# Two of the first weight loads issued from ScalarE's queue, behind a small copy that calls for its table

## The chip, the cores and the metric

The kernel runs on one core of a Trainium2 chip. The metric is the device time of one execution in microseconds, lower is better; three runs of the kernel before are shown, and one more execution with the hardware profiler on. In the profile the engines are called PE (TensorE, matmuls), PEld (TensorE's weight loads), DVE (VectorE), ACT (ScalarE), POOL (GpSimd) and SP (SyncE, which here only issues transfers); SPq is SyncE's instruction queue.

## The reference

Two branches over the same x (2048 x 512, fp32) are mixed row by row with a sigmoid gate. Branch A is a two-dimensional Fourier transform written as matmuls, of which the real part is kept. Branch B is a gated unit with a ReLU gate.

```python
def reference(A_x, A_dft_seq_re, A_dft_seq_im, A_dft_hid_re, A_dft_hid_im, B_x, B_W_gate, B_W_up, B_W_down, gate_w):
    ...
        a = jnp.einsum("bsd,ed->bse", x, dft_hid_re)
        b = jnp.einsum("bsd,ed->bse", x, dft_hid_im)
        y = jnp.einsum("ts,bse->bte", dft_seq_re, a) - jnp.einsum("ts,bse->bte", dft_seq_im, b)
    ...
        gate = jnp.einsum("bsd,df->bsf", x, W_gate)
        up = jnp.einsum("bsd,df->bsf", x, W_up)
        gate = gate * (lambda x, dt: x.astype(dt))(gate > 0, gate.dtype)
        h = gate * up
        return jnp.einsum("bsf,fd->bsd", h, W_down)
    ...
    g = _sigmoid((x * gate_w).sum(-1, keepdims=True))
    ...
    return g * a + (1 - g) * b
```

Here W_gate and W_up are 512 x 1792, W_down is 1792 x 512, and the sequence matrices are 2048 x 2048.

## The kernel before

**Arithmetic.** Each fp32 operand is split into a high part (a cast to the fp32r type) and a low part (the difference), and a product is three matmuls: high by low, low by high, high by high (`PARTS`). Most products of 2 x 2 blocks are formed with seven block products in place of eight (the tables `LEFT`, `RIGHT` and `ORDER`); the tile names carry the number of the product or of the block. In the head, product 1 needs the block "11" of x and the first column half of a weight set, product 2 the block "21" and the second column half; the products 5, 6, 3, 7, 4 need sums of blocks.

**Stages.** The matmuls that form the hidden layer come first (weight sets c = 0 to 6, each for 128 columns in both halves of gate and up, and two halves q of the rows), then the transform along the hidden dimension, then the transform along the sequence together with the down projection. The change lies in the first few microseconds.

**The planner.** Engines run their instructions in program order, and the kernel's own planner (`Plan`) writes that order. Each operation is recorded as a `Step` with a key, the number of the matmul it belongs to. `due` works back from the matmuls to a latest time of each step; `order` (line 191) then plays the steps through in its own figures: 0.5 us for an issue on SyncE or ScalarE (`ISSUE`), one line on which transfers move one behind another at 0.175/16 us for each 4 KB (1.4 us for 512 KB), landing 2.5 us behind that (`LANDING`), a cast on ScalarE 0.19 us and 0.845 ns an element, 0.035 us for a wait (`WAIT`). A transfer issued between 2.3 and 2.9 us is counted 2.3 times (`COLD`). SyncE's and ScalarE's steps are looked through some 48 deep, VectorE's and ScalarE's sorted by due time: the first that can start is taken, unless a later one can start more than 0.12 us earlier (line 224). Line 255 sorts everything by the planned start, and that is the program. Whatever the chip does, an engine then waits for its steps in this order.

**Who issues what.** `load` (line 356) issues from SyncE, `store` and `accumulate` from GpSimd. ScalarE issues no transfer. `Weights.load` (line 413) loads raw weights, half `h`, column half `n`, depth half `k`; `a_hi` (416) casts them on ScalarE into `wah`, `a_lo` (419) forms `wal` on VectorE.

**The head** (from line 1230). `warm_up` clears `gs` on VectorE (128 x 64) and runs 18 matmuls on constants. The loads are recorded, and issued by SyncE, in this order: x "11" first depth half, weight set 0 first column half and first depth half, x "11" second depth half, set 0 first column half and second depth half, set 1 first column half (both depth halves in one), x "21" whole, set 0 second column half, set 1 second column half, x "12", the other halves of the weights, x "22" and the gate's weights. On the chip a cast of a weight piece waits for its load. TensorE's order is fixed: 12 matmuls of product 1 on set 0 (six on the first depth half, six on the second), 12 of product 1 on set 1, then product 2 on set 0 and on set 1, then the others. Product 2 on a set adds into the bank of product 1, so it also waits until ScalarE has copied that bank (`evac`, the ACT COPY of 128 x 1024).

Of the kernel before, what the change touches and what calls it, by code (L numbers as in the profile page):

```python
# [8 lines left out]
F32 = mybir.dt.float32  # L9
# [5 lines left out]
P = 128  # L15
# [113 lines left out]
class Plan:  # L129
# [3 lines left out]

    MATMUL, WAIT, LANDING, COLD = 0.22667, 0.035, 2.5, 2.3

    ISSUE = {"sync": 0.5, "scalar": 0.5, "gpsimd": 0.9}

    REST = 60
# [5 lines left out]
    def op(self, key, f, *a):  # L144
        self.ops.append((key, len(self.ops), f, a))
# [45 lines left out]
    def order(self):  # L191
        todo = {}
        for s in self.steps:
            todo.setdefault(s.engine, []).append(s)
        for e in ("vector", "scalar"):
            todo[e].sort(key=lambda s: s.due)
        free = dict.fromkeys(todo, 0.0)
        late, line, live, ends = 0.0, 0.0, 0, []
        left = {b: len({id(x) for x in b.uses}) for b in self.bufs if b.kind == "unit"}
        done, begun, now = [], set(), 0.0  # L200

        turn = {s: n for n, s in enumerate(self.steps)}
        ahead = sorted(min(turn[s] for s in b.uses) for b in left if b.uses)
        while any(todo.values()):
            best = None
            for e, queue in todo.items():
                found = None
                near = queue[:1] if e == "tensor" or not queue else [*queue[:48], min(queue, key=turn.get)]
                for s in near:
                    if any(x.start is None for x in s.after):  # L210
                        continue
                    t = max(free[e], now)
                    for x in s.after:
                        t = max(t, x.end + (0 if x.engine == e else self.WAIT + 0.16 * (x.engine == "tensor")))
                    if e != "tensor":
                        t = max(t, (s.key - self.AHEAD[e]) * self.MATMUL + late)
                    new = {r.base for r in (*s.writes, *s.reads) if r.base.kind == "unit" and r.base not in begun}
                    if new:
                        short = live + bisect_left(ahead, turn[s]) + len(new) - UNITS
                        if short > 0:  # L220
                            if len(ends) < short:
                                continue
                            t = max(t, ends[short - 1])
                    if found is None or t < found[0] - 0.12:
                        found = t, s, new
                if found and (best is None or found[0] < best[0]):
                    best = found
            if best is None:
                raise ValueError(f"no way on at {len(done)}: {[(e, q[0].key, q[0].name) for e, q in todo.items() if q]}")
            t, s, new = best  # L230
            now = t
            while ends and ends[0] <= t:
                ends.pop(0)
                live -= 1
            live += len(new)
            for b in new:
                ahead.remove(min(turn[x] for x in b.uses))
            begun |= new
            todo[s.engine].remove(s)
            s.start = t  # L240
            if s.name == "dma_start":
                free[s.engine] = t + self.ISSUE[s.engine]
                line = max(line, free[s.engine]) + s.work * (self.COLD if 2.3 < t < 2.9 else 1)
                s.end = line + self.LANDING + (2.0 if "accum_op" in s.k else 0)
            else:
                s.end, free[s.engine] = t + s.work, t + s.hold
            if s.engine == "tensor" and s.key >= 0:
                late = max(late, t - s.key * self.MATMUL - 6 * self.MATMUL)
            for b in {r.base for r in (*s.writes, *s.reads) if r.base.kind == "unit"}:
                left[b] -= 1  # L250
                if not left[b]:
                    ends.append(max(x.end for x in b.uses))
                    ends.sort()
            done.append(s)
        self.steps = sorted(done, key=lambda s: s.start - 0.2 * (s.engine == "scalar"))
# [23 lines left out]
def kernel(ctx: ExitStack, tc, xP, xG, wgu, wd, cr, ci, wri, gw, out):  # L279
# [22 lines left out]
    small = ctx.enter_context(tc.tile_pool(name="small", bufs=1))  # L302

    plan = Plan()
    op, pe = plan.op, plan.pe
# [10 lines left out]

    gs = Buf(plan, "gs", [2, 32], kind="fixed", tile=small.tile([P, 2, 32], F32, name="gs"))

    gx = Buf(plan, "gx", [2, 32], kind="fixed", tile=small.tile([P, 2, 32], F32, name="gx"))

    def buf(name, shape=(2, N), dtype=F32):
# [22 lines left out]
    def E():  # L344
        return plan

    def mm(ps, w, x, start=False, stop=False):
        plan.tensor.matmul(ps, w, x, start=start, stop=stop, skip_group_check=True)
# [7 lines left out]
    def load(o, i):  # L356
        plan.sync.dma_start(o, i)
# [15 lines left out]
    def x_load(q, b, ks=slice(0, 2)):  # L373
        k, j, o = int(b[0]) - 1, int(b[1]) - 1, piece[q, b]
        return lambda: load(o[:, ks], xP[2 * q + j, k, :, ks])
# [26 lines left out]
    class Weights:  # L402
# [7 lines left out]
            self.d = buf("wd", [2, 2, 2, P], F32R)  # L410
            self.b = [[buf(f"wb{h}{x}", [2, 2, 2, P], F32R) for x in "hl"] for h in range(2)]

        def load(self, h, n=slice(0, 2), k=slice(0, 2)):
            load(self.raw[h][:, n, k], wgu[self.c, h, :, n, k])

        def a_hi(self, n=slice(0, 2), k=slice(0, 2)):
            E().scalar.copy(self.a[0][:, n, k], self.raw[0][:, n, k])
# [268 lines left out]
    def gate_store():  # L686
        for n in range(2):
            E().vector.transpose(gx[:, n], gs[:, n])
            for i in range(0, P, 32):
                load(gd[n, :, i:i + 32], gx[i:i + NT * KD, n])  # L690
# [376 lines left out]
    class Joint:  # L1067
# [5 lines left out]
        def __init__(self, ms, banks, x=2, raw=None, last=False, lead=(0, 0), own=()):  # L1073
            self.ms, self.banks, self.x, self.lead, base, wide = ms, banks, x, lead, plan.now, 12 * len(ms)
            self.w, self.c, self.s = {}, {}, buf("js")
            self.o = [buf(f"jo{p}") for p in range(2)]
            self.g = gate_row(0, (x - 2, x), base + 10)
            for n, m in enumerate(ms):
                self.lefts(m, base + 12 * n - lead[1], raw, wide)
            self.v = [buf("jv0"), buf("jv1", (N,))] if last else None  # L1080
            made = {(m, hh): self.sums(m, hh, base + 6 * hh - lead[1]) for m in own for hh in range(2)}
            if last:
                op(base - 40, lambda: load(self.v[0].all, od[x - 2, :, 0:2]))
                op(base + 20, lambda: load(self.v[1].all, od[x, :, 1]))
            order = [(y, m) for y in ORDER_Z for m in ms]
            if last:
                order[-4:] = [(y, m) for m in ms for y in ORDER_Z[-2:]]
            for n, (y, m) in enumerate(order):
                for hh in range(2):
                    self.right(m, y, hh, base + 12 * n + 6 * hh, made.get((m, hh)))  # L1090
            for y, m in order:
                for hh in range(2):
                    pe(6, self.product, m, y, hh)
                if m == ms[-1]:
                    self.evac(y, plan.now)
                elif last and y == 4:
                    op(plan.now, lambda: E().scalar.copy(self.half(1), self.bank(4, HALVES[1])))
# [131 lines left out]

    def warm_up():  # L1230
        E().vector.memset(gs.all, 0.0)
        for n in range(WARM):
            half = slice(n % 2 * (N // 2), (n % 2 + 1) * (N // 2))
            mm(ps8[:, (2, 3, 6, 7)[n // 2 % 4], half], ones[:, :P], ones, start=n in (0, 2, 4, 6), stop=True)

    NP = KF // 2
    ws = [Weights(c) for c in range(2)]
# [4 lines left out]
    halves, whole = [slice(0, 1), slice(1, 2)], slice(0, 2)  # L1242
# [6 lines left out]
    def w_half(w, n, k=whole):  # L1249
        w.a_hi(n, k)  # L1250
        w.a_lo(n, k)

    op(-100, warm_up)
    for k in halves:
        op(-99, x_load(0, "11", k))
        op(-99, ws[0].load, 0, halves[0], k)
    op(-99, ws[1].load, 0, halves[0])
    op(-99, x_load(0, "21"))
    for w in ws:
        op(-99, w.load, 0, halves[1])  # L1260
    op(-98, x_load(0, "12"))
    for w in ws:
        op(-98, w.load, 1)
# [11 lines left out]
    for n, m in enumerate((5, 6, 3, 7, 4)):  # L1275
# [3 lines left out]
        for w in ws:  # L1279
# [3 lines left out]
            else:  # L1283
                h, i = divmod(SLOT[m], 2)
# [28 lines left out]
    def prepared(c, ahead=66):  # L1313
        w = Weights(c)
        w_prep(w, plan.now, ahead)
        return w

    for c in range(2, NP):
        w = prepared(c)
# [123 lines left out]
```

## Time and profile before

| | |
|---|---|
| median of three runs | 779.66 us (779.49, 779.66, 781.6) |
| the profiled execution | 779.72 us |
| its span in the profile | 777.9 us |
| granted TensorE clock, mean | 0.999 |
| PE busy | 772.3 us, 99% of the span, 3414 matmuls |
| DVE busy | 665.5 us, 86%, 736 instructions |
| ACT busy | 425.9 us, 55%, 499 instructions |
| POOL busy | 121.5 us, 16%, 178 instructions |
| moved by the DMA engines | 205.65 MB, mean 264 GB/s |

The span runs from the first to the last instruction; the time of the execution has about 1.8 us around it. The profile's rows give a start and a duration in microseconds, the engine, the line of the kernel, the operation, and the tiles written and read (buffer numbers left out); what stands in brackets is how long the engine had been idle before, and what released it. Since the planner issues every instruction, all have line 126, and the tile names tell them apart. Matmuls are pipelined and overlap in the rows, so their pace is read from start to start. A view of the transfers gives for each load its size and the time from issue to landing.

### The profile page before, as it was taken

What the parts mean: (1) busy time and instruction counts of PE and PEld (TensorE: products, weight loads), DVE (VectorE), ACT (ScalarE), POOL (GpSimd) and SP (SyncE); (2) the same over time, 40 slices, a digit from 0 to 9 for tenths busy, and PEclk for the clock granted to TensorE, in tenths of its full rate; (3) what the DMA queues carried; (4) which work ended last, traced back from release to release, by engine and by line L of the source; (5) the groups of instructions that cost most, each with busy time, mean ns of one, the idle gap of its engine ahead of it and who ended that gap; (6) DMA issues with size and microseconds to landing.
All of it is one profiled execution on the core that took longest, in us unless ns stands there. A gap on an engine that the chain in (4) does not pass through costs nothing.

```text
span 777.9 us, 9558 instructions
## 1 busy us (share of the span) xinstructions
PE 772.3 (99%) x3414; PEld 638.3 (82%) x3414; DVE 665.5 (86%) x736; ACT 425.9 (55%) x499; POOL 121.5 (16%) x178
## 2 busy tenths in 40 slices
PE   9999999999999999999999999999999999999997
PEld 7888888888888888888888888888888888888886
DVE  6999766766778685999996999998699899699898
ACT  6666444434455443566653667547644755345791
POOL 0021333332222332211000000030002011001000
PEclk9999999999999999999999999999999999999999
DMA  9246497999897999775369789989989997999982
GB/s 324 82 150 163 162 267 227 314 300 251 229 322 281 337 408 405 276 279 187 94 208 380 267 262 389 373 172 266 310 294 206 356 306 167 284 250 305 388 278 55
DMA packets 60255, 205.65 MB, mean 264 GB/s; under 512 B 7152, under 2 KB 7664, under 8 KB 60208
## 3 DMA queue, kind: packets, MB, share of 16 engines
q1 hardware_dynamic: 37264, 122.72, 43.5%
q0 software_dynamic: 22944, 82.32, 39.2%
q8 instruction: 27, 0.44, 0.2%
q14 instruction: 20, 0.16, 0.1%
HBM read 155.45 MB, written 74.73 MB: 296 GB/s over the span
## 4 chain that ended last, share of the span: by engine, by line
PE 98%; DMA 1%; SPq 0%; ACT 0%; DVE 0%; issue 0%; DVEq 0%
PE ps L126 98%; DMA x<-xP 1%; SPq L126 0%; DVE jo L126 0%; ACT xh L126 0%; ACT wah L126 0%; DVEq L126 0%
## 5 line engine op out<-in xcount | busy, mean ns | idle before, releaser
L126 PE MATMUL ps<-ch,ll 128*128 128x512 f32 x516 | 200.7, 389 | 0.0
L126 PE MATMUL ps<-cl,lh 128*128 128x512 f32 x516 | 200.7, 389 | 0.0
L126 PE MATMUL ps<-ch,lh 128*128 128x512 f32 x516 | 200.7, 389 | 0.0
L126 ACT CAST ch<-r 128x1024 fp32r<-128x1024 f32 x80 | 82.1, 1054 | 74.1 <-DVE r L126 64.6
L126 PEld LDWEIGHTS ps<-ch,ll 128*128 128x128 f32 x516 | 96.9, 188 | 20.1
L126 PEld LDWEIGHTS ps<-cl,lh 128*128 128x128 f32 x516 | 96.9, 188 | 20.1
L126 PEld LDWEIGHTS ps<-ch,lh 128*128 128x128 f32 x516 | 96.9, 188 | 20.0
L126 DVE TENSOR_TENSOR cl<-r,ch 128x1024 fp32r<-128x1024 f32 x80 | 95.6, 1221 | 7.7 <-ACT ch L126 6.1
L126 ACT CAST ch<-hr 128x1024 fp32r<-128x1024 f32 (+1 forms) x56 | 51.8, 945 | 43.5 <-DVE hr L126 21.2
L126 DVE TENSOR_TENSOR jcl<-jc,jch 128x1024 fp32r<-128x1024 f32 x56 | 65.6, 1222 | 7.8 <-issue 3.9
L126 ACT COPY s<-ps 128x1024 f32<-128x1024 f32 (+1 forms) x52 | 46.0, 884 | 47.6 <-PE ps L126 46.3
L126 ACT CAST jch<-jc 128x1024 fp32r<-128x1024 f32 x56 | 56.2, 1052 | 16.1 <-PE ps L126 14.0
L126 DVE TENSOR_TENSOR cl<-hr,ch 128x1024 fp32r<-128x1024 f32 (+1 forms) x56 | 60.1, 1087 | 5.1 <-ACT lh L126 2.7
L126 ACT ACTIVATE ps<-ps 128x512 f32<-128x512 f32 (+1 forms) x42 | 33.0, 785 | 55.0 <-PE ps L126 52.6
L126 POOL DMA_DIRECT2D out<-z x20 | 14.6, 729 | 297.3 <-DVE z L126 290.0
L126 DVE TENSOR_TENSOR r<-r,r 128x1024 f32<-128x1024 f32 x48 | 57.6, 1220 | 0.2
L126 DVE TENSOR_TENSOR u<-ps,s 128x1024 f32<-128x1024 f32 x28 | 34.1, 1221 | 13.4 <-PE ps L126 8.8
L126 POOL DMA_DIRECT2D hd<-h x35 | 23.0, 662 | 136.9 <-DVE h L126 125.6
L126 PE MATMUL ps<-xh,wb0l 128*128 128x512 f32 x112 | 43.8, 391 | 0.0
L126 PE MATMUL ps<-xh,wb0h 128*128 128x512 f32 x112 | 43.6, 389 | 0.0
L126 PE MATMUL ps<-xl,wb0h 128*128 128x512 f32 x112 | 43.6, 389 | 0.0
L126 PE MATMUL ps<-xh,wb1l 128*128 128x512 f32 x112 | 43.6, 389 | 0.0
(161 smaller groups left out, 1536.1 us busy)
## 6 DMA issues: line engine op xcount, KB each, us to landing
hr<-hd SPq DMA_DIRECT2D x33, 512.0 KB, 5.1
jc<-td SPq DMA_DIRECT2D x32, 512.0 KB, 8.1
td<-ci POOLq DMA_DIRECT2D x24, 512.0 KB, 10.1
r<-cr SPq DMA_DIRECT2D x24, 512.0 KB, 9.5
r<-ci SPq DMA_DIRECT2D x24, 512.0 KB, 8.5
out<-z POOLq DMA_DIRECT2D x20, 512.0 KB, 7.2
l<-ad SPq DMA_DIRECT2D x18, 512.0 KB, 8.7
wr<-wgu SPq DMA_DIRECT2D x16, 512.0 KB, 8.3
```

What stands on the lines that cost most here:

```text
L126: getattr(getattr(nc, self.engine), self.name)(*map(ap, self.a), **{k: ap(x) for k, x in self.k.items()})
```

## The change

A tile `first` (128 x 32) is added. `warm_up` copies a part of the cleared `gs` into it on ScalarE, as the first step of that engine. The load of set 1's first column half and that of set 0's second column half are issued by ScalarE; the others stay on SyncE, in the same order as before among themselves. The planner gets a figure `TABLE`, 1.4 us, before which it plans no transfer on ScalarE.

```diff
+    TABLE = 1.4
...
+                    if e == "scalar" and s.name == "dma_start":
+                        t = max(t, self.TABLE)
...
+    first = Buf(plan, "first", [32], kind="fixed", tile=small.tile([P, 32], F32, name="first"))
...
-        def load(self, h, n=slice(0, 2), k=slice(0, 2)):
-            load(self.raw[h][:, n, k], wgu[self.c, h, :, n, k])
+        def load(self, h, n=slice(0, 2), k=slice(0, 2), queue=None):
+            (queue or load)(self.raw[h][:, n, k], wgu[self.c, h, :, n, k])
...
     def warm_up():
         E().vector.memset(gs.all, 0.0)
+        E().scalar.copy(first[:], gs[:, 0])
...
     for k in halves:
         op(-99, x_load(0, "11", k))
         op(-99, ws[0].load, 0, halves[0], k)
-    op(-99, ws[1].load, 0, halves[0])
+    op(-99, ws[1].load, 0, halves[0], whole, plan.scalar.dma_start)
     op(-99, x_load(0, "21"))
-    for w in ws:
-        op(-99, w.load, 0, halves[1])
+    op(-99, ws[0].load, 0, halves[1], whole, plan.scalar.dma_start)
+    op(-99, ws[1].load, 0, halves[1])
     op(-98, x_load(0, "12"))
```

## The prediction

> **What bounds the kernel now.** I read the page first, then the chain of work that ended last.
>
> ```profile
> span 777.9 us, 9558 instructions
> 3.07 6.43 DMA x<-xP
> 9.52 1.14 ACT xh L126 x2
> 10.66 0.53 ACT wah L126
> 11.23 761.70 PE ps L126 x3366
> 774.28 0.42 DVE jo L126
> ```
>
> (Columns: start, duration, what.) From 11.23 us to 772.93 us the chain is TensorE alone, and what follows, the last output tile, is untouched by the change. So the kernel is one dense stream of matmuls that began late; a change at the head moves the end by as much as it moves the start of that stream. I therefore read the first 14 us engine by engine, in order of time.
>
> ```profile
> 0.78 4.00 PE L126 MATMUL ps<-const-bfloat16-1.0 128*128 128x256 bf16 x18 [0.78 <-PEq L1436]
> 4.71 0.88 PE L126 MATMUL ps<-xh,wah 128*128 128x512 f32 x2
> 6.36 0.63 PE L126 MATMUL ps<-xh,wah 128*128 128x512 f32 x2
> 7.74 0.69 PE L126 MATMUL ps<-xh,wah 128*128 128x512 f32 x2
> 10.08 0.61 PE L126 MATMUL ps<-xh,wal 128*128 128x512 f32 x2
> 11.23 0.74 PE L126 MATMUL ps<-xh,wah 128*128 128x512 f32 x2 [0.54 <-ACT wah L126]
> ...
> 0.74 1.28 ACT L126 ACT_TABLE_LOAD   x1 [0.74 <-PEq L1436]
> 4.25 0.41 ACT L126 CAST wah<-wr 128x256 fp32r<-128x256 f32 x1 [2.23 <-DMA wr<-wgu]
> 5.50 0.41 ACT L126 CAST wah<-wr 128x256 fp32r<-128x256 f32 x1 [0.84 <-DMA wr<-wgu]
> 7.24 0.71 ACT L126 CAST wah<-wr 128x256 fp32r<-128x256 f32 x2 [1.34 <-DMA wr<-wgu]
> 7.94 1.00 ACT L126 COPY ps<-ps 128x1024 f32<-128x1024 f32 x1
> 9.52 1.14 ACT L126 CAST xh<-x 128x512 fp32r<-128x512 f32 x2 [0.58 <-DMA x<-xP]
> 10.57 0.61 ACT L126 CAST wah<-wr 128x512 fp32r<-128x512 f32 x1
> ```
>
> Call the pieces by what they feed. Product 1 of weight set 0 takes 12 matmuls: six with the first half of the depth (x11a, w0a), six with the second (x11b, w0b). Then 12 with set 1 (w1, one load), then product 2, which needs x21 and the second column half of set 0 (w0'). The rows show these at 4.71, 6.36, 7.74 and 11.23 us. The step from 7.74 to 10.08 us is ten matmuls, so 0.23 us each. A stream without a stop from 4.71 us would reach product 2 at 4.71 + 24 x 0.23 = 10.23 us; it got there at 11.23. **The head's stalls after the first matmul are therefore worth 1.0 us**, and that is the ceiling of what earlier data for these products can give, since the first matmul waits for w0a, which the change leaves where it was.
>
> When each piece lands is its issue plus the time to landing:
>
> ```profile
> 0.74 0.38 SPq L126 DMA_DIRECT2D x<-xP  x1
> 1.18 0.42 SPq L126 DMA_DIRECT2D wr<-wgu  x1
> 1.65 0.42 SPq L126 DMA_DIRECT2D x<-xP  x1
> 2.12 0.91 SPq L126 DMA_DIRECT2D wr<-wgu  x2
> 3.07 0.43 SPq L126 DMA_DIRECT2D x<-xP  x1
> 3.54 0.91 SPq L126 DMA_DIRECT2D wr<-wgu  x2
> ...
> x<-xP SPq DMA_DIRECT2D x1, 256.0 KB, 2.6
> wr<-wgu SPq DMA_DIRECT2D x1, 128.0 KB, 3.0
> x<-xP SPq DMA_DIRECT2D x1, 256.0 KB, 3.5
> wr<-wgu SPq DMA_DIRECT2D x1, 128.0 KB, 3.4
> wr<-wgu SPq DMA_DIRECT2D x1, 256.0 KB, 4.6
> x<-xP SPq DMA_DIRECT2D x1, 512.0 KB, 6.4
> wr<-wgu SPq DMA_DIRECT2D x1, 256.0 KB, 6.6
> wr<-wgu SPq DMA_DIRECT2D x1, 256.0 KB, 6.8
> ...
> DMA  0000000000000000000000029548599998999988
> q1 hardware_dynamic: 177, 0.48, 100.2%
> ```
>
> In order of issue: x11a 3.3 us, w0a 4.2, x11b 5.1, w0b 5.5, w1 (second of the pair at 2.12, so issued at about 2.6) 7.2, x21 9.5, w0' 10.1, w1' (issued at about 4.0) 10.8. As a curve of KB landed: 384 at 4.2 us, 640 at 5.1, 768 at 5.5, 1024 at 7.2, 1536 at 9.5, 1792 at 10.1. The last two rows are DMA activity in the first 3 us, in 40 slices, and the queue's share from 5 to 7 us. From 5 to 7 us the engines stand at 100%: there they, and not the issuing, set the landings.
>
> **The change part by part.** *The small copy.* Table load and copy: the load already stands at 0.74 and ends at 2.02 us, so the copy adds no load. Its length from two rows of ScalarE: 128x256 takes 0.41 us, and 128x512 takes 0.61, so 0.2 + 32 x 0.0008 = 0.23 us (bounds: 0.11, the memset below, and 0.41, the cast). It waits for the memset of gs, done at 0.94 us.
>
> ```profile
> 0.83 0.11 DVE L126 MEMSET gs<- 128x64 f32 x1 [0.83 <-PEq L1436]
> 5.16 0.43 DVE L126 CAST xh<-x 128x512 fp32r<-128x512 f32 x1
> ```
>
> *Two issues on ScalarE.* From 2.25 us, at 0.38 to 0.46 us each as on SyncE (0.91 for two), they end at about 3.1 us. ScalarE is idle until 4.25 us, waiting for w0a, so copy and issues cost nothing; without that cover they would cost 1.1 us. In the planner both sort ahead of ScalarE's first cast. Nothing on ScalarE is queued behind them that could have begun earlier.
>
> *SyncE.* Two issues fewer: x21 is issued 0.47 us earlier (2.59 for 3.07), w1' about 0.9 us earlier. As the DMA engines are full from 3 us on, an earlier issue moves no landing by itself: 0, at most 0.47 for x21.
>
> *Two transfers on another queue.* On SyncE's queue w1 came behind x11b and w0b. Now its bytes start when ScalarE's queue does: the first bytes of x11a moved in slice 23 of 40, 1.73 us, so 1.0 us behind the issue, and those of w1 at about 2.25 + 1.0 = 3.25 us. By then x11a and most of w0a are through. From there w1 and w0' stand **beside** x11b, w0b and x21. No row shows two queues at once at this place. If they share by bytes, x11b (256 KB) is through when 384 + 512 = 896 KB have landed, by the curve 5.5 + 1.7 x 128/256 = 6.35 us, for 5.1 before. w1 lands at that time too (7.2 before). Then w0b (128 KB) with as much of w0': 1152 KB, 7.2 + 2.3 x 128/512 = 7.8 us, for 5.5. If they take turns row by row, w0b has rows of 1 KB against 2 KB, so 1280 KB: 8.35 us.
>
> *The order on ScalarE.* The planner writes it. In its own figures SyncE issues at 0, 0.5, 1.0 and 1.5, ScalarE at 1.4 (TABLE). Its single line of transfers thus takes w1 ahead of w0b: the line stands at 2.25 after x11b, 2.95 after w1, 3.30 after w0b, so landings (2.5 later) of 5.45 and 5.80. ScalarE takes the step that can start earliest, unless one with an earlier due time is within 0.12. The first cast of w1 (5.49) beats that of w0b (5.84) by more than that. So ScalarE's order becomes: w0a, **first half of w1, w0b**, second half of w1. (The same arithmetic on the kernel before gives w0b, then w1, then both casts of x21, then w0', as the rows show.) The six matmuls on w0b now cannot start before w1 has landed as well, whichever queue is served first: x11b, w0b and w1 together make 1024 KB, 7.2 us. That is a lower bound for the cast of w0b as long as the curve holds.
>
> *The sum.* Before, w0a landed at 4.2 and its matmul began at 4.71: 0.5 us for the cast and two hand-overs. With w0b at 7.8 the second six matmuls start at 8.3 us (6.36 less a few hundredths before), and product 2 follows 18 x 0.23 = 4.14 later, at 12.44. By then x21 (1792 KB, about 10.1 us) and w0' are there, and ScalarE has had the evacuation (1.0) and the casts of x21 (1.14) behind 9.7 us. The cast of x11b on VectorE (0.43) ends before 7 us. So 12.44 - 11.23 = **1.2 us later**. Lower end, w0b at 7.2: 7.7 + 4.14 = 11.84, 0.6 later. Upper end, 8.35: 12.99, 1.8 later. I take the middle, sharing by bytes, since most pieces in question have 2 KB rows. The saved stalls at 7.74 and 11.23 are in this sum already. The dense stream keeps the rest: nothing behind it waits, so it isn't won back.
>
> The Trainium skill, "DMA: Bandwidth & Descriptors", section "Queues, rings and completion order", says that each DMA engine goes round the queues that have work, packet by packet, and under "Issuing engines are not separate DMA queues" that a second issuing engine saves only issue time. By that rule the sharing above holds and the time is 780.9; by the opposite, a second queue with a rate of its own, it is the first rival. No row here shows two of these queues busy together, while the share of 100.2% agrees that no engine has room.
>
> The profiled execution took 779.72 us (span 777.9), the median of the runs is 779.66, which is 0.06 less and small beside all terms here. 779.72 + 1.2 = 780.9.
>
> **The rivals.** *Two queues move more than one (faster).* The engines moved only 768 KB between 5.5 and 9.5, wide of what they do next: 256 KB of w0' in 0.6 us. If slow answers rather than engine time set that stretch, two queues overlap them. At 256 KB per 0.7 us (w1') the 640 KB behind w0a land by 5.95 us, the second six start at 6.45, product 2 at 10.6: 0.6 faster, 779.1; with no stall at all 10.23, 778.7. Against it: the 100% share. It decides from 1024 KB landed before about 6.5 us.
>
> *Nothing changes.* Between the two: 1024 KB at about 6.6 us gives 7.1 + 4.14 = 11.24, so 779.7.
>
> *SyncE's queue is served first.* Then w1 comes behind x21, at 1536 KB, 9.5 us; its first cast ends at about 9.9, w0b's at 10.3, product 2 at 14.5: 3.2 later, 782.9. For it only the order of issue of the pieces; x21 is issued after w1, so it is not likely.
>
> *TensorE cools down.* The warm-up's 256 columns took 4.00/18 = 0.22 us, as long as 512 columns afterwards: half speed for the first 4.0 us. The forecast leaves TensorE idle from 6.1 to 8.3 us. Were it set back for as long again, 2.0 us are lost on top: 782.9. The Trainium skill, "TensorE: Matmul & The Clock Gate", section on the HAM clock gate, puts the fall behind an idle window of about 3.4 us, more than my gap; no row here shows a fall from a gap of this length.
>
> *The copy doesn't hold the issues back.* Then w1 starts at about 1.7 us and delays w0a too, but w0b still comes with 1280 KB: 781.5, inside the forecast.
>
> **How the numbers follow.** Forecast (0.6 to 1.8 later, the last case with it): 0.57, own range 780.3 to 781.5. Within 0.3 us: 0.14. Faster by up to 1.0: 0.19. Later than 1.8: 0.10, of which 0.07 beyond 0.3%. A range of 778.9 to 782.1 leaves out the best of the third case and most of the last, under 0.2 in all. A measurement of this kernel tells 0.3%, 2.34 us, from no change. The ceiling of 1.0 leaves nothing for "faster by over 0.3%" but an accident in the planner's order further on: 0.02. Slower: 0.07. Within: 0.91.
>
> **What would show it.** Right: two issues on ScalarE between 2.2 and 3.2 us; x11b landing after 5.6 us and w0b after 7; ScalarE casting half of w1 before w0b; a gap on TensorE of over 1 us ahead of the seventh real matmul, and none ahead of set 1 or product 2; the dense stream from product 2 at about 12.4. Wrong: w0b cast before 6.5 us, product 2 before 11.2, a stop in the stream after 14 us, or matmuls of 0.46 us behind the gap.

## The result, and the profile after

| | before | after |
|---|---|---|
| median of 12 runs each, us | 779.58 | 780.77 |
| the profiled execution, us | 779.72 | 780.76 |
| its span, us | 777.9 | 778.8 |

The ratio of the times is 1.0015, with a 95% interval from 1.0008 to 1.0022: 1.2 us slower, which is inside the 0.3% named above as no change but clear of the noise of these runs. The forecast was 780.9, 1.2 later.

The page of the changed kernel shows a queue that was not there before, ScalarE's, with the two moved loads and nothing else (packets, MB, share of 16 engines):

```profile
span 778.8 us, 9560 instructions
...
q10 hardware_dynamic: 288, 0.52, 0.2%
```

The chain of work that ended last, after:

```profile
2.12 5.28 DMA wr<-wgu
...
7.42 0.41 ACT wah L126
...
7.88 765.77 PE ps L126 x3384
...
775.00 0.43 DVE jo L126
```

Before, the dense stream of matmuls hung on x21, landing at 9.5 us. Now it hangs on w0b, the load issued at 2.12 us, and begins at the seventh real matmul. TensorE's rows, after:

```profile
5.10 1.22 PE L126 MATMUL ps<-xh,wah 128*128 128x512 f32 x2 [0.31 <-ACT wah L126]
6.12 0.86 PE L126 MATMUL ps<-xl,wah 128*128 128x512 f32 x2
6.82 0.63 PE L126 MATMUL ps<-xh,wal 128*128 128x512 f32 x2
7.88 0.73 PE L126 MATMUL ps<-xh,wah 128*128 128x512 f32 x2 [0.43 <-ACT wah L126]
...
12.29 0.62 PE L126 MATMUL ps<-xh,wah 128*128 128x512 f32 x2
...
17.74 0.39 PE L126 MATMUL ps<-xh,wb0l 128*128 128x512 f32 x1
```

The second six start at 7.88 us (6.36 before), product 2 at 12.29 (11.23), product 5 at 17.74. ScalarE's rows, after, say what that start waited for:

```profile
0.74 1.28 ACT L126 ACT_TABLE_LOAD   x1 [0.74 <-PEq L1443]
0.98 0.86 ACTq L126 DMA_DIRECT2D wr<-wgu  x2
2.04 0.22 ACT L126 COPY first<-gs 128x32 f32<-128x32 f32 x1
4.64 0.71 ACT L126 CAST wah<-wr 128x256 fp32r<-128x256 f32 x2 [2.38 <-DMA wr<-wgu]
7.42 1.24 ACT L126 CAST wah<-wr 128x256 fp32r<-128x256 f32 x3 [2.07 <-DMA wr<-wgu]
```

The pair at 4.64 is w0a and the first half of w1; then ScalarE stood idle for 2.07 us until w0b was there. And the loads, by issue in order of time (x11a, w1, w0a, w0', x11b, w0b, x21; KB, us from issue to landing):

```profile
x<-xP SPq DMA_DIRECT2D x1, 256.0 KB, 2.9
wr<-wgu ACTq DMA_DIRECT2D x1, 256.0 KB, 3.3
wr<-wgu SPq DMA_DIRECT2D x1, 128.0 KB, 3.4
wr<-wgu ACTq DMA_DIRECT2D x1, 256.0 KB, 5.3
x<-xP SPq DMA_DIRECT2D x1, 256.0 KB, 5.4
wr<-wgu SPq DMA_DIRECT2D x1, 128.0 KB, 5.3
x<-xP SPq DMA_DIRECT2D x1, 512.0 KB, 6.2
```

With their issues at about 0.75, 0.98, 1.18, 1.41, 1.66, 2.12 and 2.60 us, they land at 3.6 (x11a), 4.3 (w1), 4.6 (w0a), 6.7 (w0'), 7.1 (x11b), 7.4 (w0b) and 8.8 us (x21). Against before, w1 came 2.9 us earlier, w0' 3.4 and x21 0.7, while x11b and w0b came 1.9 us later. The two pieces that are needed next were overtaken by two that are needed later.

Both queues had loads under way at that time, but they did not share evenly. From 3.0 to 3.5 us ScalarE's queue (q10) had the engines nearly to itself (packets, MB, share of 16 engines):

```profile
q10 hardware_dynamic: 97, 0.19, 98.1%
q1 hardware_dynamic: 10, 0.01, 6.7%
```

The pieces above land in the order in which they were issued, whichever engine issued them. What the second queue changed is the time of issue: before, w1 went out at 2.59 us and w0' at 3.54, now at 0.98 and 1.40.

### The profile page after: what moved, and what is told of

Its sections match the earlier page's. It is cut to its first block, busy times and chain, and to the rows that moved or that the text cites. A ratio compares the mean times of both kernels' runs of the same rounds, so it can differ in the third digit from the quotient of the medians.

```text
span 778.8 us, 9560 instructions
## 1 busy us (share of the span) xinstructions
PE 772.8 (99%) x3414; PEld 638.8 (82%) x3414; DVE 665.4 (85%) x736; ACT 425.1 (55%) x500; POOL 121.2 (16%) x178
## 4 chain that ended last, share of the span: by engine, by line
PE 98%; DMA 1%; DVE 0%; SPq 0%; ACT 0%; issue 0%; DVEq 0%
PE ps L126 98%; DMA wr<-wgu 1%; DVE jo L126 0%; SPq L126 0%; ACT wah L126 0%; DVEq L126 0%
```

## The experiments

Theory S: the two loads on ScalarE's queue take the DMA engines' time from x11b and w0b, and TensorE waits for these. Theory O: ScalarE's changed order of casts, half of w1 ahead of w0b, costs the time. Theory C: the copy, the table and the issues on ScalarE cost it. Every ratio below is to the kernel before, run beside it, with a 95% interval; where a profile is read it is that of one execution.

**Without the copy.**

```diff
     def warm_up():
         E().vector.memset(gs.all, 0.0)
-        E().scalar.copy(first[:], gs[:, 0])
```

> The changed kernel without the small copy; ScalarE's first instructions are then the two issues, and the table load comes behind them. Theory S (sharing: w1 and w0' move beside and ahead of x11b and w0b on the DMA engines, so w0b lands late): issues at about 0.75 and 1.2 us, table load over before the first cast (about 4.6 us), second six matmuls at 7.6 to 7.9 us, time 780.4 to 781.0 as with the copy. Rival C (the copy and the table cost the time): 779.6, as before the change.

781.07 us, ratio 1.0017 (1.0008 to 1.0026): the time stays without the copy, so theory C falls for the copy and the place of the table load. The issues themselves fall inside time in which ScalarE waits for its first weights anyway (2.38 us of it in the rows above). ScalarE's rows show what the copy does:

```profile
0.74 0.89 ACTq L126 DMA_DIRECT2D wr<-wgu  x2
1.66 1.28 ACT L126 ACT_TABLE_LOAD   x1 [1.66 <-PEq L1442]
```

Here the table load stands ahead of the first copy or cast on ScalarE. Without the copy that is a cast behind the two issues; with it, the load goes first. In neither case does an issue wait for the load or the copy to end: with the copy the first issue is at 0.98 us, the load ends at 2.02 and the copy starts at 2.04. (The profiled execution was the shortest of the eleven, 779.91, and does not show the wait of theory S: its chain hangs on w0a, which landed at 5.4 us. The first real matmul came at 5.90 and the second six followed without a stop at 7.40. What the longer executions waited for, this one profile does not show.)

**One load alone.**

```diff
-    op(-99, ws[0].load, 0, halves[1], whole, plan.scalar.dma_start)
+    op(-99, ws[0].load, 0, halves[1])
```

> One part alone: only w1 is issued by ScalarE, w0' is back on SyncE behind x21. Theory S: 256 KB fewer stand ahead of w0b, so it lands at about 6.6 us in place of 7.4, the second six start at about 7.0, product 2 at about 11.2, time 779.3 to 779.9. Rival O (ScalarE's new order of casts, first half of w1 ahead of w0b, costs the time): the order is the same as in the changed kernel, so 780.6 to 781.

779.5 us, ratio 0.9997 (0.9988 to 1.0005).

```diff
-    op(-99, ws[1].load, 0, halves[0], whole, plan.scalar.dma_start)
+    op(-99, ws[1].load, 0, halves[0])
```

> The other part alone: only w0' is issued by ScalarE, w1 is back on SyncE behind w0b. Theory S: w0b again has 256 KB fewer ahead of it, second six at about 7.0 us, product 2 at about 11.2 to 11.5 (w1 lands behind w0b, about 7.5, in time), time 779.3 to 780.0. Rival O: w1 is no longer cast ahead of w0b, 779.6; a time of 780.6 or more would speak against both.

779.78 us, ratio 1.0001 (0.9992 to 1.001). First six, second six and product 2, with only w1 moved:

```profile
5.50 0.73 PE L126 MATMUL ps<-xh,wah 128*128 128x512 f32 x2 [0.82 <-ACT wah L126]
...
6.99 0.62 PE L126 MATMUL ps<-xh,wah 128*128 128x512 f32 x2
...
11.12 0.62 PE L126 MATMUL ps<-xh,wah 128*128 128x512 f32 x2
```

and with only w0' moved:

```profile
5.39 0.73 PE L126 MATMUL ps<-xh,wah 128*128 128x512 f32 x2 [0.61 <-ACT wah L126]
...
6.88 0.62 PE L126 MATMUL ps<-xh,wah 128*128 128x512 f32 x2
...
11.22 0.61 PE L126 MATMUL ps<-xh,wah 128*128 128x512 f32 x2
```

The starts are where theory S put them (7.0 and 11.2), and so are the times, but not for its reason. w0b landed at 6.0 and 5.9 us, not at 6.6, and the second six did not wait for it. In both runs the chain hangs on w0a, which landed at 5.0 and 4.9 us (4.2 before), so the first real matmul came 0.7 to 0.8 us later than before; then TensorE reached product 2 nearly without a stop. One load alone thus delays the first matmul by about as much as it takes out of the stops behind it, and costs nothing that can be measured; both together bring w0b too late as well and cost 1.2 us. In the first of the two runs the casts are in the order that theory O blames, and the time did not rise.

**The order of the casts alone.** In the changed kernel it is put back:

```diff
         self.read()
+        cast = [s for s in self.steps if s.engine == "scalar" and s.writes[0].base.name == "wah"]
+        cast[2].after.add(cast[1])
+        cast[3].after.add(cast[1])
         self.due()
```

> The changed kernel with ScalarE's order of the casts put back (w0b ahead of both halves of w1). Theory S: w1 lands at 4.3 us there, long before w0b, so its cast ahead of w0b cost nothing: second six at about 7.9, product 2 at about 12.3, time 780.5 to 781. Rival O: 779.6.

780.63 us, ratio 1.0012 (1.0003 to 1.0021), the second six at 7.91 us, behind w0b's landing at 7.4 as before this edit, and product 2 at 12.16. Theory O falls for this kernel: w1 had landed at 4.3 us, so nobody waited for its cast. In the kernel before, where w1 lands behind w0b, the same order was forced by the opposite edit (`cast[1].after.add(cast[2])`):

> The kernel before, all loads on SyncE, with one edit: the planner must put the cast of the first half of w1 ahead of that of w0b on ScalarE. The disputed cost by itself: w1 lands at 7.2 us there, so w0b's cast ends at about 7.9, the second six start at about 8.0 in place of 6.4 and product 2 at about 12.1, time 780.3 to 780.7. If the order is harmless, 779.6.

781.11 us, ratio 1.0016 (1.0007 to 1.0025), but not by the way that was expected. In the profiled execution (779.99 us) w1 landed early, at 6.1, and product 2 came at 11.18 us, no later than before. The chain ran on VectorE instead:

```profile
16.22 0.70 DVE wb0l L126
...
17.05 756.14 PE ps L126 x3342
```

With one forced pair, the planner also wrote another order for VectorE: a second sum of weights stands ahead of the low part that product 5 needs, which then ends at 16.92 us. Product 5 starts at 17.05 (16.85 before). The changed kernel has this order on VectorE too, but there product 2 is so late that product 5, at 17.74 us, did not wait for VectorE; in the profile without the copy, with the same order, it did not at 17.06 either. So the order of casts was not isolated by this run; its eleven executions lie between 779.99 and 782.49, and what the longer ones did the single profile does not show.

**The issues held back until the copy is done.** The copies write into the places where the loads will land:

```diff
-        E().scalar.copy(first[:], gs[:, 0])
+        for w, n in ((ws[1], 0), (ws[0], 1)):
+            E().scalar.copy(w.raw[0][:, n, 0, 0, :32], gs[:, 0])
```

> The copy made to hold the issues: two small copies write into the places where w1 and w0' will land, so the transfers have to wait for them; issues at 2.3 us or later. This is the case that the prediction's sum was made for: x11b less late (about 6 us), w0b at 7.2 to 7.8, second six at 7.6 to 8.3, product 2 at 11.8 to 12.4, time 780.1 to 780.9. If the early issue alone is what costs the time, w0b lands before 6.5 us and the time is 779.6 or less.

780.68 us, ratio 1.0013 (1.0004 to 1.0022): the time of the prediction's case, by another path. In the profiled execution (780.28, the shortest of the eleven) w0b landed at 6.6 us, the second six start at 7.15 and product 2 at 11.41, all earlier than expected. At product 2 the two loads now cost 0.2 us, where they cost 1.1 with the early issue. But ScalarE's rows show a wait in a bad place:

```profile
2.28 0.86 ACTq L126 DMA_DIRECT2D wr<-wgu  x2
...
8.93 0.62 ACT L126 CAST wah<-wr 128x512 fp32r<-128x512 f32 x1 [1.52 <-DMA wr<-wgu]
9.45 1.01 ACT L126 COPY ps<-ps 128x1024 f32<-128x1024 f32 x1
10.40 1.13 ACT L126 CAST xh<-x 128x512 fp32r<-128x512 f32 x2
```

The cast of w0' waits 1.52 us for its load, and behind it on ScalarE stand the bank's evacuation and the casts of x21. From there the chain runs through VectorE to product 5, at 17.28 us (16.85 before).

**The pieces on two queues in the order of need.** ScalarE issues w0a and w0b ahead of its table load, SyncE the rest:

```diff
-    TABLE = 1.4
+    TABLE = 0.25
...
     for k in halves:
         op(-99, x_load(0, "11", k))
-        op(-99, ws[0].load, 0, halves[0], k)
-    op(-99, ws[1].load, 0, halves[0], whole, plan.scalar.dma_start)
+        op(-99, ws[0].load, 0, halves[0], k, plan.scalar.dma_start)
+    op(-99, ws[1].load, 0, halves[0])
     op(-99, x_load(0, "21"))
-    op(-99, ws[0].load, 0, halves[1], whole, plan.scalar.dma_start)
+    op(-99, ws[0].load, 0, halves[1])
```

> Two queues with the pieces in the order in which they are needed: ScalarE issues w0a and w0b (TABLE 0.25, so ahead of its table load), SyncE x11a, x11b, w1, x21, w0', w1' and the rest. If two queues move more bytes and only the order of the pieces was wrong: w0b lands before 5.5 us, no stop on TensorE after its first matmul, product 2 at 10.2 to 10.6, time 778.5 to 779.1. If the engines' rate is that of the kernel before: w1 at about 7.2, x21 at 9.5, product 2 at 10.8 to 11.2, time 779.2 to 779.6.

779.39 us, ratio 1.0003 (0.9994 to 1.0012): no difference that can be told. Three of its eleven executions took 780.99 to 781.32 us, the others 779.24 to 779.46. In the profiled execution, one of the eight shorter ones:

```profile
5.12 0.73 PE L126 MATMUL ps<-xh,wah 128*128 128x512 f32 x2 [0.59 <-ACT wah L126]
...
10.88 0.62 PE L126 MATMUL ps<-xh,wah 128*128 128x512 f32 x2
...
16.33 0.39 PE L126 MATMUL ps<-xh,wb0l 128*128 128x512 f32 x1
```

After its first matmul TensorE reaches product 2 in 5.76 us, close to the 5.52 of a stream without a stop, and the data of product 2 are early, x21 at 7.8 us. But x11a and w0a now share the engines too, w0a lands at 4.6 in place of 4.2, and the first matmul starts 0.4 us later. Product 5 comes 0.5 us earlier than before, too little for these medians. Neither case of the expectation holds as it stood: time and product 2 are those of the second, but w1 (6.6 us) and x21 landed sooner than it says, and w0b (5.7) later than the first says. With x21 on ScalarE's queue as well (an added `queue` argument of `x_load`):

> As the run before it, and x21 issued by ScalarE too, behind w0b. Sharing by bytes: x21 (512 KB) moves beside w1 and w0', so w1 lands later (about 7.5 us, set 1 would start late by some 0.3 to 0.8) and x21 earlier or at the same time; product 2 at 10.4 to 11.2, time 778.7 to 779.6. If the queues do not hinder each other: 778.5.

780.25 us, ratio 1.0012 (1.0003 to 1.0021), later than expected. x21 and w1, issued within 0.01 us of each other, moved side by side and landed at 8.2 and 8.0 us. Here the queues did share, packet for packet and not byte for byte: from 5.5 to 7.0 us ScalarE's queue moved 96 packets with 0.38 MB, SyncE's 99 packets with 0.18 MB. The late w1 cost TensorE 0.2 us (24 matmuls to product 2 in 5.96 us, for 5.76), and product 2 started at 11.33. The time was set behind it. Product 5 waited until 17.48 us (16.33 in the run before), and the chain to it runs through ScalarE and VectorE:

```profile
14.03 0.60 ACT g L126
...
16.82 0.61 DVE wb0l L126
```

The planner had put the activation g ahead of the cast that product 5's sums need. So this run says little about the queues by its time.

**A second profiled execution of each kernel.**

> One more look at the kernel before, for how far its head varies from execution to execution. If the curve of landings of the first profile is typical: w1 at 7.2 us, x21 at 9.5, product 2 at 11.2, time 779.6. If w1's late landing there was chance: w1 near 6.1 (as in the run with only ScalarE's order changed), x21 still above 9, product 2 near 11, the same time within 0.3 us.

779.83 us; w1 at 7.0 us, x21 at 9.2, close to the curve of landings in the prediction (only in the run with w1 cast first had w1 landed at 6.1). TensorE's rows:

```profile
4.59 1.22 PE L126 MATMUL ps<-xh,wah 128*128 128x512 f32 x2
...
7.07 0.63 PE L126 MATMUL ps<-xh,wah 128*128 128x512 f32 x2
...
11.28 0.73 PE L126 MATMUL ps<-xh,wah 128*128 128x512 f32 x2
```

Here the first six matmuls took 7.07 - 4.59 = 2.48 us, against 1.65 in the first profile, yet product 2 started at about the same time. TensorE stood still for less than 0.1 us ahead of it: x21 had landed at 9.2, ScalarE was free of the bank's copy at 9.6, and its casts of x21 and w0' then ended at 11.2. So the 1.0 us of stalls in the prediction belongs to the first execution; here slow matmuls filled most of it.

> One more look at the changed kernel. Theory S: x11b and w0b land at 7.0 to 7.5 us again, second six matmuls at 7.9, product 2 at 12.2 to 12.4, product 5 at about 17.7. The first matmuls took 0.5 us each in the first profile and 0.23 in the run with the casts put back; which of the two appears here is open, and it should not move product 2.

780.39 us; x11b 6.5 (sooner than expected), w0b 7.4, second six 7.90, product 2 12.11, product 5 17.56. The wait for w0b is the same, though the pieces around it moved by up to 1.3 us.

**How long the warm-up must be.** On the kernel with the order of need:

```diff
-    WARM = 18
+    WARM = 10
```

> The two queues in need order with 10 warm-up matmuls in place of 18, so that TensorE is idle from about 3.0 us to its first real matmul at 5.1. If the clock that the array runs at hangs on its being kept busy: real matmuls at 0.45 us apiece for up to 3.4 us, product 2 at 12 to 12.6 in place of 10.9, time 780.4 to 781.1. If not: 779.4 as with 18.

781.39 us, ratio 1.0019 (1.001 to 1.0027). TensorE's rows:

```profile
5.41 1.22 PE L126 MATMUL ps<-xh,wah 128*128 128x512 f32 x2 [2.34 <-ACT wah L126]
...
9.85 0.83 PE L126 MATMUL ps<-xh,wal 128*128 128x512 f32 x2
10.52 0.63 PE L126 MATMUL ps<-xh,wah 128*128 128x512 f32 x2
...
13.25 0.62 PE L126 MATMUL ps<-xh,wah 128*128 128x512 f32 x2
```

From 5.41 to 9.85 us ten matmuls took 0.44 us each, nearly twice the usual 0.23, after 2.34 us of idle time; product 2 came at 13.25, 2.4 us later than with 18. Both product 2 and the time are somewhat beyond what was expected.

> The two queues in need order with 22 warm-up matmuls, so that TensorE has no gap before its first real matmul (4.3 to 5.1 us with 18). If the three executions out of eleven near 781.3 with 18 were ones in which the array fell back to the slower clock in that gap, they are gone, all executions near 779.3. If they have another cause, some stay.

779.5 us, ratio 0.9994 (0.9985 to 1.0003). Its executions run from 779.15 to 780.14 and none is near 781.3, which agrees with slow first matmuls as the cause of those three, but it is not shown. None of the three was profiled, the kernel before has a few such executions too (781.37 and 781.32 among the 33 beside the first runs), and with 22 warm-up matmuls the first two real ones were still slow (1.02 us from 5.35 to 6.37). Against the kernel before it is no gain that can be told.

## Why the prediction was right, step by step

**"One dense stream of matmuls that began late"**: held. The chain is TensorE from 7.88 us to the end.

**The small copy** was put at 0.23 us and took 0.22, at no cost, as the run without it shows.

**"Two issues on ScalarE. From 2.25 us"**: wrong. They went out at 0.98 us. I let an issue wait for the instruction ahead of it; the row of the issues lies inside the table load's. So the rival "the copy doesn't hold the issues back" came true in that part, and with it its delay of w0a (4.6 us, for 4.2), though not its time of 781.5.

**Two transfers on another queue**: that the moved loads make x11b and w0b late, and TensorE wait for w0b, held; the chain hangs on w0b at 7.4 us in all three profiles with both loads issued early behind the table load (the changed kernel twice, and with the casts put back). The size is partly luck. w0b was put at 7.8 us, with 1152 KB landed by then. It landed with 1280 KB, since the issues went out 1.3 us sooner; by the prediction's own curve that is 8.35 us, but the data moved faster than on that curve, and it was 7.4. Two errors nearly cancel. In the run that holds the issues back, which is the case of the sum, w0b landed at 6.6 and product 2 came 0.2 us later, not 1.2. Sharing by bytes is not what the traces show: from 3.0 to 3.5 us the second queue had nearly all, and where two queues did share they took turns by packet.

**The order on ScalarE**: forecast rightly, and harmless. "The six matmuls on w0b now cannot start before w1 has landed as well" is true but bound nothing, because w1 was in 3.1 us ahead of w0b.

**The sum**: second six at 7.88 (8.3 forecast), product 2 at 12.29 (12.44). The gap of over 1 us ahead of the seventh matmul was only 0.43, since the first six began at 5.10 (4.71 before) and the first three of them were slow. The 18 matmuls between took 4.41 us, not 4.14: the second six also waited for the low parts, which VectorE could only form once the late pieces were there (0.3 us of TensorE's loads stood behind them).

**"Nothing behind it waits, so it isn't won back"**: wrong by 0.34 us. TensorE's stream ended 0.72 us later (7.88 + 765.77 against 772.93), while product 2 was 1.06 later. Of the difference, 0.17 was won back between product 2 and product 5 (5.62 us before, where product 5 started at 16.85; 5.45 after): the first pair of product 2, which stood behind a stop before, took 0.58 us then and 0.46 after. The rest was won back at about 22 to 25 us, where TensorE's weight loads before waited twice for VectorE (us in total, times, longest). After, they do not:

```profile
PEld ps L126 <- DVE wb0l L126: 0.5, 2, 0.3
```

The time of 780.9 against 780.77 is thus partly luck: product 2 was put 0.15 us too late and 0.34 us of winning back were left out, while the profiled executions differ by 1.04 us, 0.32 more than the stream's end, in the rows behind it and around the span. The medians differ by 1.19.

**The rival "two queues move more than one"**: its half about the rate was right, and my argument against it, "the 100% share", was none. In steps of one microsecond, before (the last two columns are the DMA share and GB/s):

```profile
5.00:6.00 1.00, 1.00 (x5) 0.82 (x5) 0.92 (x3) 0.41 (x1) 0.00 (x0) 1.00 1.30 257
6.00:7.00 1.00, 1.00 (x6) 0.82 (x5) 0.65 (x2) 0.00 (x0) 0.00 (x0) 1.00 0.70 219
7.00:8.00 1.00, 1.00 (x5) 0.69 (x5) 0.32 (x1) 0.76 (x3) 0.00 (x0) 1.00 0.82 205
```

and after:

```profile
5.00:6.00 1.00, 0.90 (x2) 0.81 (x3) 0.43 (x1) 0.35 (x2) 0.00 (x0) 1.00 0.96 262
6.00:7.00 1.00, 1.00 (x4) 0.76 (x4) 0.00 (x0) 0.00 (x0) 0.00 (x0) 1.00 1.05 412
7.00:8.00 1.00, 0.57 (x3) 0.13 (x3) 0.86 (x2) 0.58 (x2) 0.00 (x0) 1.00 1.02 402
```

The share counts the whole time of a packet in the step in which it starts, so 1.30 means packets that run on into the next step; 0.70 and 0.82 are not gaps. Over the three steps the engines were nearly as busy before as after (0.94 and 1.01), but moved 227 GB/s in place of about 360. The packets themselves took longer: 170 ns on the mean and up to 1.9 us before, 96 ns and up to 0.5 after. A share of 100% thus holds slow answers as well, and could not speak against a rival that supposed them. The changed kernel had 2048 KB landed at 9.5 us, where the kernel before had 1536. It moved more and still lost, because the extra bytes were not those that TensorE waited for.

**"TensorE cools down"**: half speed was seen, in the first three matmuls after (0.5 us each) and far more with a short warm-up, but ahead of the gap, not behind it. The rival itself was not put to the test at the length that it supposed: in place of 2.2 us TensorE stood still for 0.43 us, 1.16 with the casts put back, and the rows behind show no half speed. In the changed kernel the slow first matmuls cost nothing, since the second six waited for w0b anyway; the casts put back and the first pairs at 0.29 us gave the same 7.9 us.

## What to carry to other kernels

Moving a load to a second queue changes when it is issued, and with that its place among all loads. In every profile here the first eight loads landed in the order of their issue over both queues; only loads issued within 0.2 us of each other changed places. So a load that was moved out of the long queue went ahead of everything that still waited there to be issued. Write down the order of issue against the order of need before counting saved issues, and look at the first piece as well: a load alone on the second queue made w0a late. And the small copy ahead of the issues did not hold them back, while copies that write where the transfers will land did.

## What the runs showed of the hardware

- An issue on ScalarE goes out while the table load ahead of it runs (0.98 us against 0.74 to 2.02).
- With two queues the first 1536 KB landed at 7.4 us (only w1 moved), 7.8 (order of need) and 8.2 (x21 moved as well), with one queue at 9.1 to 9.5 in three executions (the kernel before twice, and with w1 cast first). With one queue the packets that started from 5 to 8 us took 166 to 191 ns on the mean, the longest of each execution 1.9 to 2.2 us; in the eleven profiles with two queues it was 87 to 121 ns and at most 0.9 us. Why stays open; no run was made for it.
- Two queues with loads under way at the same time were served unevenly (98.1% of the engines' time to one, 6.7% to the other, from 3.0 to 3.5 us in the changed kernel) or packet for packet (96 and 99 packets from 5.5 to 7.0 us, with 0.38 and 0.18 MB, x21 on ScalarE's queue). What decides between the two was not tried.
- The first real matmuls run at half speed in some executions and not in others of the same kernel: the first six took 2.48 and 1.65 us in two profiles of the kernel before. A pause of 2.34 us ahead of them after a short warm-up gave ten such matmuls and 2.0 us. The granted clock of the profile does not show it: it reads 1.00 in the steps of 2 us in which these ten ran.
